# Two-batch attention feeding a dense layer pair on one Trainium2 core: idle matrix products in short bf16 pieces, the first phi tile in three column parts, smaller q loads, the last output tile in two halves, and a new order of the steps

## The chip, the core and the metric

The kernel runs on one core of a Trainium2 chip. The core has a matrix engine (PE, with its weight loads listed apart as PEld), a vector engine (DVE), an activation engine (ACT), GpSimd (POOL), and a queue engine (SP) that here only issues DMAs. Each of them works through its own instructions strictly in the order in which they were written; what one needs of another it waits for with a semaphore. Sixteen DMA engines carry the transfers between HBM and SBUF. Matrix results go to PSUM, which has eight banks; only PE, DVE and ACT reach them. The metric is the device time of one execution in microseconds (us); lower is better. A difference of 0.2% of 655.1 us, 1.3 us, is about what a measurement of this kernel can tell from no change.

## The reference

Eight batches of eight heads, 576 rows each. `phi` makes 32 memory slots a head out of the keys and values, queries attend to the slots, and the result goes through two dense layers with a leaky ReLU between them. The products are wanted in float32.

```python
def _attn_ref(q, k, v, phi):                 # q, k, v: (8, 8, 576, 64), phi: (8, 8, 576, 32)
    a = np.exp(phi - np.max(phi, axis=2, keepdims=True))
    a = a / (np.sum(a, axis=2, keepdims=True) + 1e-09)
    k_m = np.einsum('bhsm,bhsd->bhmd', a, k)
    v_m = np.einsum('bhsm,bhsd->bhmd', a, v)
    scores = 1.0 / np.sqrt(q.shape[-1]) * np.matmul(q, k_m.transpose(0, 1, 3, 2))
    attn = np.exp(scores - np.max(scores, axis=-1, keepdims=True))
    attn = attn / (np.sum(attn, axis=-1, keepdims=True) + 1e-09)
    return np.matmul(attn, v_m)

def _moe_ref(x, w_in, w_out):                # x: (4608, 512), w_in: (512, 2048), w_out: (2048, 512)
    h = x @ w_in
    return np.maximum(0.01 * h, h) @ w_out   # w_in and w_out arrive as float64
```

## The kernel before

The product with the value slots is folded into the first layer: per batch the slots `v_m` (transposed: `vT`) are multiplied with a quarter of `w_in` (`fold_products`, L1007), and the attention weights `a` then go straight through that folded matrix (`w_mem`). So a row of the output costs one "up" product (`a` by folded weights, 128 hidden units at a time), a leaky ReLU on ACT, and one "down" product with `w_out`.

The work is written as small named steps, and two long strings, `OPENING` (L39) and `LATER` (L67), list the steps in the order in which they are issued. Each engine gets its own instructions in that order: a step that stands early in the string stands early on every engine that it uses, and nothing is reordered after that. The names are:

- `a0.` to `a7.` are the eight batches. `phi`, `k`, `v`, `kv`, `q0`, `q1` issue loads on SP. `A1` is the column maximum of phi on DVE, `A2` its transposition on PE, `A3` and `B0` spread the maximum over all rows (DVE, PE). `B1` subtracts it (DVE, L658), `B2` is the exponential (ACT, L664), `B3` sums the exponentials (DVE, L680 to L683). `C1` makes the slots on PE (L698): in batch 0 `C10` is the keys' part and `C11` the values'. `C2` and `C30` make the reciprocal of the sums, `C3k` scales the key slots (ACT), `C31` the value slots (DVE, L754). `D10` and `D3` transpose the key slots (PE, ACT), `D11` and `D5` the value slots, `C4`, `D2`, `D4` bound their size. `Q0` and `Q1` transpose q on DVE (L845). `E10` and `E1` are the scores on PE (L887), `E20` to `E22` copy and transpose them (DVE, L908). `S01` to `S08` is the softmax over the slots for one chunk of the scores, `S11` to `S18` that of the other chunk.
- `i0.` to `i3.` and `o0.` to `o3.` are quarters of `w_in` and `w_out`, each in three pieces: `ld` loads a piece as float64 words into one of eight slots of 6 KB a partition, `y` (ACT), `h` (ACT or DVE, by `OPENING_ACT`) and `t` (DVE, L406) make float32 of it, `b` sums its squares (ACT, 2048 columns).
- `u0.` to `u7.` are the first group of 384 output rows: `P` is an up product (L1114), `V` its leaky ReLU (ACT, L1121), `O` a down product of three row tiles (L1186). `f01.1` is a fold and `f01.2` its two copies into `w_mem`. Capital letters (`P8.0` and on) are groups 1 and 2, `W` the later folds, small letters (`p`, `v`, `d`, `c`, `l`, `s`, `x`) the rest of the rows.
- `z.n` are n idle products (L1384): a matrix of ones times itself, whose result nobody reads.

All loads, and nearly all stores, are issued by SP. Eight semaphores serve the loads in turn, so that a load is issued when the load eight places ahead of it has landed and its slot is free.

The last group has one tile of 128 rows. `down_tile` (L1324) adds its 16 pieces of three products, 512 columns wide, into one PSUM bank; `store` with `last=True` (L1166) scales the left half on ACT and the right half on DVE and sends four stores of 32 rows, two on SP's queue and two on ACT's:

```python
        if last:
            nc.scalar.activation(ob[:, 0:EH], po[:, 0:EH], AF.Copy, scale=so)
            nc.vector.tensor_scalar_mul(ob[:, EH:], po[:, EH:], so)
```

PSUM tiles come from three pools: `ps_a` (three banks, attention and folds), `ps_h` (two, up products), `ps_o` (three, down products).

Of the kernel before, what the change touches and what calls it, by code (L numbers as in the profile page):

```python
# [66 lines left out]
LATER = """  # L67
W01.h1 a2.phi a2.kv2 a2.kv1 o0.s0 W01.h0 a2.A1 Z0.0 o0.s1 a2.kv0 a2.A2 W01.l0 o0.m0 W01.l1 o0.m1
o0.n0 o0.n1 Z0.1 o0.s2 i0.k1 W11.p Z0.2 P8.0 P8.1 V8.0 a2.kv3 W11.h1 P9.0 o0.s3 V8.1 W11.h0 C8 P9.1
L8 W11.l1 V9.0 o1.k0 a2.A4 W11.l0 V9.1 O8.0 W02.h0 o1.l0 W02.h1 C9 o1.k1 O8.1 W02.l1 o1.k2 W02.l0  # L70
o0.m2 L9 o0.m3 W12.p o1.l2 o1.l1 P10.0 W12.h0 o0.n2 P10.1 V10.0 i0.k0 W12.l0 W12.h1 P11.0 o1.s0
V10.1 i0.k2 W12.l1 O9.0 V11.0 C10 o1.m0 o0.n3 L10 P11.1 o1.s1 O9.1 W03.h1 o1.n0 W03.h0 o3.s3 V11.1
P12.0 o1.m1 O10.0 C11 V12.0 o1.n1 L11 P12.1 o1.s2 O10.1 o1.m2 W03.l1 o1.s3 V12.1 W03.l0 a2.A3 o1.n2
o2.k0 C12 W13.p o2.k2 o2.l0 W13.h1 P13.0 W13.h0 W13.l1 P13.1 W13.l0 V13.0 o2.k1 L12 V13.1 O11.0
o1.m3 P14.0 o2.l1 V14.0 C13 o2.s0 P14.1 L13 o2.m0 O11.1 a2.B10 V14.1 o1.n3 o2.n0 o2.s1 P15.0 a2.B20
C14 o2.m1 O12.0 o2.s2 V15.0 o2.n1 o2.m2 a2.C10 L14 P15.1 o2.s3 a2.B3 O12.1 o2.l2 a2.q0 V15.1 o2.n2
o3.s0 a2.q1 o3.k1 o3.k0 o3.l1 P16.0 P16.1 o3.k2 O13.0 V16.0 C15 o2.m3 o3.s1 O13.1 V16.1 C16 o3.l0
o3.s2 o3.m1 a2.C2 a2.C30 i0.l1 o3.l2 o3.m2 P17.0 L15 o3.m3 o3.n3 O14.0 V17.0 L16 a3.phi P17.1 a2.Q0
a2.C3k V17.1 C17 O14.1 o3.n1 a2.D10 i0.l0 a2.Q1 a2.D3 P18.0 O15.0 V18.0 a2.C31 o3.n2 i0.l2 O15.1
o3.m0 P18.1 a2.E1 a2.E22 a2.E3 a3.kv3 i1.k0 L17 a2.E21 a2.E23 V18.1 i1.l0 P19.0 a2.E20 a2.C4 i1.k1  # L80
Z1.2 a3.kv2 P19.1 a2.D11 a2.S01 C18 Z1.1 a3.kv1 Z1.0 a2.S02 L18 V19.0 O16.0 i1.k2 a2.D2 a2.D4
a3.kv0 a2.S03 i1.l2 O16.1 a2.D5 a2.D6 a2.S04 V19.1 P20.0 C19 O17.0 O17.1 o2.n3 V20.0 L19 P20.1
V20.1 i1.l1 C20 i2.k0 P21.0 W20.p a2.S05 i2.k1 O18.0 W20.h0 V21.0 W20.h1 i2.k2 P21.1 L20 O18.1
W20.l1 V21.1 W20.l0 C21 i2.l0 W21.p a2.S06 P22.0 W21.h1 W21.h0 i2.l1 O19.0 V22.0 o3.n0 i2.l2 W21.l0
i3.k1 P22.1 O19.1 i3.k0 W22.p V22.1 a3.A1 i3.k2 L21 a3.A2 W22.h0 P23.0 W22.h1 O20.0 V23.0 a2.S07
P23.1 a3.A4 O20.1 V23.1 a2.S08 i3.l2 C22 i3.l0 W22.l1 C23 W21.l1 O21.0 i3.l1 L23 p0.0 W23.p v0.0
p0.1 W23.h0 p0.2 L22 a3.A3 W23.h1 a3.B10 O21.1 W22.l0 v0.1 a3.B20 W23.l1 a3.C10 O22.0 os2 a3.B3
v0.2 a3.q0 W23.l0 a4.phi a3.C2 p0.3 a3.C30 a3.q1 O22.1 v0.3 a3.C3k s0 c0.0 a3.C31 l0.0 c0.1 a3.D10
l0.1 p1.0 p1.1 a3.D11 v1.0 O23.0 v1.1 a3.C4 p1.2 a3.D3 v1.2 p1.3 a3.Q0 O23.1 v1.3 p2.0 Z2.0 Z2.1 s1
d0.0 Z2.2 p2.1 v2.0 d0.1 v2.1 a3.D2 a4.A1 a3.D4 c1.0 d0.2 c1.1 p2.2 l1.0 d0.3 v2.2 a3.D5 d0.4 a4.A2  # L90
p2.3 a4.A4 p3.0 a3.Q1 a3.D6 l1.1 d0.5 v2.3 a3.E1 a3.E22 d0.6 a3.E3 c2.0 s2 c2.1 p3.1 a3.E23 v3.0
d1.0 v3.1 a3.E20 d1.1 a3.E21 W30.p l2.0 a3.S01 os3 d1.2 a4.kv3 W30.h0 p3.2 W30.h1 a4.kv1 d1.3 v3.2
a4.kv0 d1.4 W30.l0 d1.5 l2.1 W30.l1 p3.3 a3.S02 W31.p a4.kv2 v3.3 c3.0 d1.6 W31.h0 s3 W31.h1 p4.0
a3.S03 p4.1 v4.0 d2.0 v4.1 c3.1 d2.1 a4.A3 l3.0 d2.2 p4.2 d2.3 v4.2 a3.S04 d2.4 d2.5 a4.B10 a3.S05
p4.3 W31.l1 v4.3 p5.0 l3.1 a3.S06 v5.0 d2.6 a4.B20 d3.0 a3.S07 p5.1 W31.l0 a4.C10 s4 v5.1 a3.S08
d3.1 x3.p a4.q0 c4.0 a4.B3 p5.2 d3.2 c4.1 d3.3 x3.0 v5.2 d3.4 p5.3 l4.0 v5.3 x3.1 c5.0 l4.1 x3.2 s5
d3.5 d3.6 p6.0 x3.3 p6.1 l5.0 v6.0 d4.0 p6.2 a4.q1 v6.1 c5.1 d4.1 d4.2 z3.1 a5.phi d4.3 p6.3 l5.1
v6.2 v6.3 d4.4 a4.C2 a4.C30 d4.5 d4.6 p7.0 p7.1 a4.Q0 d5.0 a4.C3k s6 a4.D10 c6.0 a4.D3 l6.0 v7.0
v7.1 a4.Q1 c6.1 d5.1 a4.C31 d5.2 l6.1 p7.2 d5.3 v7.2 d5.4 a4.C4 a5.A1 d5.5 d5.6 d6.0 p7.3 p8.0 z3.0
d6.1 a4.E1 a4.E22 d6.2 a4.E3 a5.kv2 v7.3 c7.0 s7 a5.kv0 p8.1 v8.0 v8.1 a4.E20 a5.kv3 c7.1 a4.E21  # L100
a4.E23 l7.1 p8.2 a5.kv1 d6.3 a4.D11 v8.2 d6.4 a4.D2 a4.D4 p8.3 d6.5 a4.S01 l7.0 a4.S02 v8.3 p9.0
a4.D5 W32.p s8 d6.6 W32.h0 W32.h1 p9.1 W32.l0 v9.0 d7.0 W32.l1 v9.1 d7.1 a4.D6 x4.p os4 c8.0 d7.2
c8.1 p9.2 x4.0 d7.3 v9.2 a4.S03 d7.4 x4.1 p9.3 l8.0 x4.2 d7.5 v9.3 W33.p c9.0 l8.1 d7.6 W33.h1
# [1381 lines left out]
```

## Time and profile before

| | us |
|---|---|
| median of three runs | 655.1 |
| the three runs | 654.94 to 655.29 |
| span of the profiled execution, first to last instruction | 652.3 |
| PE busy in the span | 637.4 (98%) |
| DVE busy | 516.2 (79%) |
| ACT busy | 392.7 (60%) |
| POOL busy | 29.1 (4%) |

The profiled execution has no time of its own beside its span; the median lies 2.8 us above the span. The profile's page lists the busy time of each engine, the span in 40 slices, the chain of work that ended last (followed backwards from the last instruction), and groups of instructions by source line. The trace behind it can be asked for a timeline of each engine, for the chain in order of time, for waits, and for sums in chosen windows. A row of the timeline has the start, the duration, the engine, the line, the operation, the tiles written and read, the shape and the count, and in brackets how long the engine was idle before it and what ended that. Several like instructions are merged into one row.

### The profile page before, as it was taken

Reading aid. Unit: us, or ns where it says so; the run is one execution under the profiler, and the core shown is the slowest. Engines: PE = TensorE matmul, PEld = TensorE weight load, DVE = VectorE, ACT = ScalarE, POOL = GpSimd, SP = SyncE. Lnnn points to the kernel's source line nnn. Section 1 sums busy time; section 2 is a strip of 40 time slices with the busy share of each in tenths; the row PEclk is TensorE's granted clock in tenths of the full one; section 3 lists DMA queues with packets and bytes.
Section 4 is the critical chain, followed back from the end, with each engine's and each line's share of the span. In section 5 each row is a group of like instructions: output and inputs, shape, how many; then the busy total and the mean of one; then the engine's idle time right before and its main releaser. Section 6 shows DMA issues by size and latency. Waiting matters only on the chain.

```text
span 652.3 us, 17093 instructions
## 1 busy us (share of the span) xinstructions
PE 637.4 (98%) x7256; PEld 478.2 (73%) x7256; DVE 516.2 (79%) x863; ACT 392.7 (60%) x671; POOL 29.1 (4%) x37
## 2 busy tenths in 40 slices
PE   7899999999999999999999999999999999999997
PEld 3445545675545778888888888887878888889883
DVE  5875789998997899899969975889887897575641
ACT  2797878765463555557546565655675566565543
POOL 0010031000001001001000010000010001000000
PEclk8799999999999999999999999999999999999999
DMA  9989823105601654431154011064104110010102
GB/s 281 404 312 326 261 68 92 39 11 100 195 2 32 135 156 64 115 112 38 28 122 147 1 33 43 18 127 146 34 18 84 21 28 23 13 30 5 34 2 50
DMA packets 85309, 61.16 MB, mean 94 GB/s; under 512 B 61936, under 2 KB 68336, under 8 KB 85232
## 3 DMA queue, kind: packets, MB, share of 16 engines
q1 hardware_dynamic: 85136, 59.94, 32.8%
q8 instruction: 57, 0.93, 0.6%
q10 hardware_dynamic: 96, 0.13, 0.1%
q14 instruction: 20, 0.16, 0.1%
HBM read 50.59 MB, written 9.45 MB: 92 GB/s over the span
## 4 chain that ended last, share of the span: by engine, by line
PE 97%; DVE 1%; ACT 1%; issue 0%; POOL 0%; ACTq 0%; DVEq 0%; POOLq 0%
PE po L1297 32%; PE ph L1229 22%; PE po L1186 16%; PE ph L1114 8%; PE ph L1297 5%; PE pa L1020 4%; PE pa L698 3%; PE pa L1387 2%; PE po L1331 1%; PE pa L861 1%; PE pa L887 1%; ACT wi L1245 1%; PE pa L344 0%; PE po L698 0%; PE pa L777 0%
## 5 line engine op out<-in xcount | busy, mean ns | idle before, releaser
L1297 PEld LDWEIGHTS <-arena 128*128 128x128 f16 x2184 | 209.8, 98 | 32.0 <-issue 8.8
L1245 ACT ACTIVATE wi<-ph,g_sc 128x256 f32<-128x256 f32 (+1 forms) x224 | 99.3, 466 | 164.5 <-PE ph L1229 156.2
L1229 PE MATMUL ph<-a,w_mem 128*128 128x256 f16 (+3 forms) x1440 | 145.3, 246 | 2.9 <-ACT wi L1245 2.9
L1229 PEld LDWEIGHTS <-w_mem 128*128 128x128 f16 x1440 | 114.6, 98 | 17.8 <-issue 6.3
L1297 PE MATMUL po<-arena 128*128 128x256 f16 x936 | 122.1, 273 | 0.0
L1297 PE MATMUL po<-wo,arena 128*128 128x256 f16 x936 | 122.1, 273 | 0.0
L1186 PE MATMUL po<-wo,arena 128*128 128x512 f16 (+1 forms) x384 | 110.4, 434 | 0.0
L1274 DVE TENSOR_TENSOR arena<-arena 128x1024 f16<-128x1024 f32 x52 | 63.5, 1222 | 22.4 <-ACT arena L1270 22.4
L1274 DVE TENSOR_TENSOR arena<-wi,arena 128x768 f16<-128x768 f32 (+1 forms) x60 | 54.7, 911 | 10.1 <-ACT arena L1270 10.1
L1266 DVE TENSOR_TENSOR arena<-wi 128x256 f32<-128x256 f32 x104 | 40.4, 430 | 25.6 <-ACT wi L1245 25.1
L1270 ACT CAST arena<-arena 128x1024 f16<-128x1024 f32 x52 | 54.5, 1047 | 8.1 <-DVE arena L1266 8.0
L1114 PE MATMUL ph<-a,w_mem 128*128 128x192 f16 (+2 forms) x304 | 51.9, 317 | 0.7 <-DVE a L953 0.7
L1186 PEld LDWEIGHTS <-arena 128*128 128x128 f16 x288 | 27.8, 98 | 29.9 <-issue 0.6
L1270 ACT CAST arena<-wi 128x768 f16<-128x768 f32 (+1 forms) x60 | 46.6, 777 | 1.5
L1266 DVE TENSOR_TENSOR arena<-wi,arena 128x256 f32<-128x256 f32 x104 | 45.7, 440 | 1.8
L1297 PE MATMUL ph<-wo,arena 128*128 128x256 f16 x312 | 42.6, 273 | 0.0
L985 POOL TENSOR_TENSOR a<-t,a 128x1024 f16<-128x1024 f32 (+2 forms) x16 | 21.5, 1360 | 432.9 <-ACT a L980 432.9
L1186 PEld LDWEIGHTS po<-wo,arena 128*128 128x128 f32 x96 | 17.7, 190 | 21.4 <-issue 19.0
L1020 PE MATMUL pa<-wi,vT 64*32 64x512 f16 (+1 forms) x704 | 28.9, 420 | 0.4 <-ACT vT L805 0.4
L1121 ACT ACTIVATE arena<-ph,g_sc 128x384 f32<-128x384 f32 x32 | 18.5, 582 | 15.6 <-PE ph L1114 15.3
L1053 ACT ACTIVATE w_mem<-pa 128x512 f16<-128x512 f32 x40 | 22.7, 596 | 8.4 <-PE pa L1020 7.4
L1114 PEld LDWEIGHTS <-w_mem 128*128 128x128 f16 x240 | 20.7, 98 | 9.7 <-issue 3.6
(216 smaller groups left out, 757.8 us busy)
## 6 DMA issues: line engine op xcount, KB each, us to landing
out_dram<-obs SPq DMA_DIRECT2D x142, 64.0 KB, 1.7
arena<-in_k_dram SPq DMA_DIRECT2D x28, 288.0 KB, 4.5
arena<-in_v_dram SPq DMA_DIRECT2D x28, 288.0 KB, 5.3
arena<-in_q_dram SPq DMA_DIRECT2D x96, 72.0 KB, 2.8
arena<-in_moe_w_in_dram SPq DMA_DIRECT2D x12, 512.0 KB, 9.3
arena<-in_moe_w_out_dram SPq DMA_DIRECT2D x8, 768.0 KB, 6.8
arena<-in_phi_dram SPq DMA_DIRECT2D x7, 576.0 KB, 5.3
arena<-in_q_dram SPq DMA_DIRECT2D x4, 576.0 KB, 8.7
```

Of the source, the lines that this page charges most:

```text
L698: nc.tensor.matmul(var["pk"][g][hh * M:(hh + 1) * M, cs], ld["phi"][rows, hh, j, :], ld["kv", hh][rows, kinds[0]:kinds[-1] + 1, j, :], sta ...
L985: nc.gpsimd.tensor_tensor(piece(lo, tb), piece(t2, tb), piece(hi, tb), ALU.subtract)
L1020: nc.tensor.matmul(pf[g][cols, :], lhs, rhs, start=(n == 0), stop=(n == len(passes) - 1), tile_position=(g * D, hh * M),)
L1053: nc.scalar.activation(tiles(halves(w16(b, j), g)[:, 0]), w(g), AF.Copy, scale=ws)
L1114: nc.tensor.matmul(ph[:, t0:t0 + n * SB], lhs, rhs, start=(m == 0), stop=(m == len(seq) - 1))
L1186: nc.tensor.matmul(po, lhs, rhs, start=(f == 0 and m == 0), stop=(f == NQ * NF - 1 and m == len(seq) - 1),)
L1229: nc.tensor.matmul(ph[:, t0:t0 + n], lhs, rhs, start=(m == 0), stop=(m == len(seq) - 1))
L1245: nc.scalar.activation(dst, ph, AF.Prelu, scale=g_sc2[:, j:j + 1], alpha=SLOPE)
L1266: nc.vector.tensor_tensor(gt[:, x], y, z, op)
L1270: nc.scalar.copy(dst[:, 0], src)
L1274: nc.vector.tensor_tensor(dst[:, 1], src, dst[:, 0], ALU.subtract)
L1297: nc.tensor.matmul(acc, g[:, x, s, u], rhs, start=(h == 0 and j == 0 and u == 0 and m == 0), stop=(j == NQ - 1 and u == 1 and m == 2), ski ...
```

## The change

Idle products are now bf16: the 128 float32 ones are read as 256 bf16 values, each product is 512 columns wide, and its PSUM tile comes from `ps_h` in place of `ps_a`. The opening has 12, 4, 12 and 4 of them where it had 4, 1, 3 and 1 in float32. Phi of batch 0 is subtracted and exponentiated in three column parts (2, 3 and 4 of its 9 column blocks) in place of two (5 and 4). The factor 1/8 on the key slots moves from a DVE instruction of `C30` to the copy in `D3`. Loads of q for batches 0 and 1 take two heads a DMA: eight DMAs in place of four. The last tile's 16 pieces become 32 of half the width in two PSUM banks; the left half is scaled on ACT and stored while the right half is still being multiplied; each half is stored with two DMAs of 64 rows by 256 columns, one from SP, one from ACT. `OPENING` is reordered throughout, of `LATER` the first 45 steps and the tail.

```diff
-            nc.sync.dma_start(
-                t, q[b].rearrange("(hh g) (p j) d -> g p hh j d", g=NG, j=NJ)[g]
-            )
+            src = q[b].rearrange("(hh g) (p j) d -> g p hh j d", g=NG, j=NJ)[g]
+            for hh in range(0, HP, 2):
+                nc.sync.dma_start(t[:, hh:hh + 2], src[:, hh:hh + 2])
...
-        half = (0, (KJ + 1) // 2, KJ) if b == 0 else (0, KJ)
+        half = (0, 2, 5, KJ) if b == 0 else (0, KJ)
...
             nc.vector.reciprocal(r, r)
-            nc.vector.tensor_scalar_mul(r2[:, 1], r, 1.0 / float(D) ** 0.5)
...
-                nc.scalar.copy(kT, var["pkT"])
+                nc.scalar.activation(kT, var["pkT"], AF.Copy, scale=1.0 / float(D) ** 0.5)
...
+    def store_half(G, h, po):
+        ob, cs = obs[:, h * E:h * E + EH], slice(h * EH, (h + 1) * EH)
+        if h:
+            nc.vector.tensor_scalar_mul(ob, po[:, 0:EH], row_scale(G, 0))
+        else:
+            nc.scalar.activation(ob, po[:, 0:EH], AF.Copy, scale=row_scale(G, 0))
+        rows = out.rearrange("(b x j) e -> b j x e", b=B, j=JT)
+        (b, x0), n = next(columns(G, 0)), P // 32
+        for y in range(0, n, n // 2):
+            eng = nc.sync if y == 0 else nc.scalar
+            src = ob[32 * y:32 * (y + n // 2)]
+            eng.dma_start(rows[b, x0 // 32 + y:x0 // 32 + y + n // 2, :, cs], src)
...
-            pos[G] = [ps_o.tile([P, E], F32, name="po")]
+            pos[G] = [ps_o.tile([P, E], F32, name="po") for _ in range(2)]
+        h, i = i // NF, i % NF
...
-                pos[G][0], g[:, x, i], wo_s[j][:, y, i * E:(i + 1) * E],
+                pos[G][h][:, 0:EH], g[:, x, i],
+                wo_s[j][:, y, i * E + h * EH:i * E + (h + 1) * EH],
...
     def idle_products(n):
-        pi = ps_a.tile([P, NF, P], F32, name="pa")
+        pi = ps_h.tile([P, NF, P], F32, name="ph")
         for _ in range(n):
             nc.tensor.matmul(
-                pi, ones, ones.unsqueeze(1).broadcast_to([P, NF, P]), start=True, stop=True
+                pi, halves_of_one[:, :P], halves_of_one.unsqueeze(1).broadcast_to([P, NF // 2, 2 * P]),
+                start=True, stop=True,
             )
...
-c55.1 l55.1 d54.1 d54.2 d54.3 d55.0 d55.1 d55.2 d55.3 end
+c55.1 l55.1 d54.1 d54.5 d54.2 d54.6 d54.3 d54.7 d55.0 d55.1 d55.2 d55.3 end.0 d55.4 d55.5 d55.6
+d55.7 end.1
```

What the new order does at three places, engine by engine (a row is a line of the kernel, the operation, output and inputs, and the shape).

PE between the scores of batch 0 (L887) and the values' part of its slots (L698, after the change L700). Before, three idle products in float32:

```order
L887 MATMUL pa<-wi_87,kT 32x192 x24
L887 MATMUL pa<-wo_91,kT 32x192 x24
L1387 MATMUL pa<-ones 128x512 x3
L698 MATMUL po<-wo_92,wi_88 32x64 x2
L698 MATMUL po<-wo_93,wi_88 32x64 x2
```

With the change, sixteen in bf16, each with a weight load of its own, into a bank of `ps_h`:

```order
L887 MATMUL pa<-wi_87,kT 32x192 x24
L887 MATMUL pa<-wo_91,kT 32x192 x24
L1398 LDWEIGHTS ones
L1398 MATMUL ph<-ones 128x512
...
L700 MATMUL po<-wo_92,wi_88 32x64 x2
L700 MATMUL po<-wo_93,wi_88 32x64 x2
```

The idle products stand in the same place; they no longer take a bank that the score copies of DVE must free first.

DVE after the score copies, in the softmax of the first chunk of batch 0 (`t_308`, after the change `t_319`). Before, `x_v` (step C31, which needs PE's value slots) stands ahead of the sums (L940, step S04):

```order
L908 STREAM_TRANSPOSE t_308<-pa 128x384
L928 TENSOR_REDUCE tm<-t_308 128x12
L754 TENSOR_SCALAR x_v<-po,r_228 128x64 x2
L940 TENSOR_REDUCE ts__420<-t_308 128x24
L941 TENSOR_SCALAR ts__420<-ts__420 128x24
L942 RECIPROCAL ts__420<-ts__420 128x24
L945 TENSOR_TENSOR t_308<-t_308,ts__420 128x768
L953 STREAM_TRANSPOSE a<-t_308 128x768
```

With the change:

```order
L940 TENSOR_REDUCE ts__354<-t_319 128x24
L941 TENSOR_SCALAR ts__354<-ts__354 128x24
L942 RECIPROCAL ts__354<-ts__354 128x24
L754 TENSOR_SCALAR x_v<-po,r_247 128x64 x2
L945 TENSOR_TENSOR t_319<-t_319,ts__354 128x768
L762 TENSOR_REDUCE l_450<-x_v 128x2
L339 TENSOR_REDUCE m_453<-l_450 128x1
L341 TENSOR_SCALAR mdiag<-ident,m_453 128x128
L953 STREAM_TRANSPOSE a<-t_319 128x768
```

The sums now stand ahead of `x_v`, and the three instructions of step C4 (L762, L339, L341) ahead of the transposition that gives the attention weights `a`.

ACT at the end of the program. Before, the scaling of the left half and two stores of 32 rows by 512 columns:

```order
L1270 CAST arena<-wi_89 128x256
L1245 ACTIVATE wi_89<-ph,g_sc_101 128x128 x2
L1270 CAST arena<-wi_89 128x256
L1170 ACTIVATE obs<-po,osc 128x256
L1164 DMA out_dram<-obs 32x512 x2
L1480 UNCONDITIONAL_BRANCH
```

With the change:

```order
L1279 CAST arena<-wi_89 128x256
L1254 ACTIVATE wi_89<-ph,g_sc_101 128x128 x2
L1279 CAST arena<-wi_89 128x256
L1177 ACTIVATE obs<-po,osc 128x256
L1183 DMA out_dram<-obs 2x32x256 x2
L1493 UNCONDITIONAL_BRANCH
```

ACT's two stores are now one for each half, and each covers two blocks of 32 rows by 256 columns; SP issues two more of the same shape.

More of the change, by code (lines that the diff above doesn't have):

```diff
@@ new lines @@
+u3.P1 a1.B0 u3.V1 o2.y2 a1.B10 o2.t1 a0.D4 a1.kv3 a1.B20 i1.b i3.ld0 a1.B3 o2.t2 i3.h0 u3.O0 i3.y1
+u4.P0 i3.h1 a1.C10 a1.C2 a1.C30 a1.q1 u2.V1 a1.C31 a1.C4 u2.O1 o0.b a1.C3k u4.P1 i3.y0 o3.ld0 a1.D10
+a1.D2 i3.t0 a1.D11 a1.D5 a1.Q1 a1.D3 a1.D4 u4.V1 u4.V0 u3.O1 a1.q0 u5.P1 u5.P0 a1.Q0 a0.S18 i3.t1
+i3.ld2 a1.E1 i3.h2 i2.b a1.E21 i3.y2 u4.O0 u5.V0 o1.b a1.E20 i3.t2 a1.S01 a1.S02 u5.O0 u5.V1 o3.ld2
+o0.s0 a1.E22 o3.y0 a2.phi i3.b o3.ld1 ci.1 ci.2 f03.1 o3.h2 o3.h1 o3.h0 a1.S03 a1.S11 ci.3 f03.2
@@ L63 @@
 }
-IDLE = (1, 2, 3, 4)
+IDLE = (1, 2, 3, 4, 6, 8, 12)
 LATER = """
[L68 to L78, printed above, removed]
@@ L85 @@
[L85 to L90, printed above, removed]
@@ new lines @@
+v13.0 d11.0 a5.B10 v13.1 d11.1 c12.1 x5.p d11.2 l12.1 p13.2 d11.3 x5.0 l12.0 v13.2 a5.B20 d11.4
+p13.3 x5.1 a5.C10 x5.2 v13.3 c13.0 s13 d11.5 a5.q0 l13.0 d11.6 c13.1 p14.0 x5.3 p14.1 v14.0 d12.0
+a5.q1 p14.2 a5.B3 d12.1 d12.2 l13.1 a5.C2 a5.C30 d12.3 a5.Q0 v14.1 v14.2 d12.4 a6.phi a5.C3k p14.3
+d12.5 v14.3 a5.D10 a5.D3 c14.0 d12.6 s14 p15.0 a5.C31 v15.0 l14.0 c14.1 p15.1 d13.0 a5.Q1 l14.1
+v15.1 d13.1 z5.1 d13.2 p15.2 d13.3 v15.2 d13.4 d13.5 d13.6 p15.3 p16.0 a5.E1 a5.E22 a5.C4 a5.E3
+a6.kv2 a5.E23 a5.E20 d14.0 v15.3 z5.0 c15.0 s15 p16.1 a6.kv3 a5.D11 v16.0 a6.kv0 v16.1 a5.D2 a5.D4
@@ L1154, in row_scale, with send @@
         return osc_t[:, bs[0] // 2:bs[0] // 2 + 1]
-    def send(G, t, ob, last=False):
+    def send(G, t, ob):
         for y, (b, x) in enumerate(columns(G, t)):
-            rows, eng = out[b * S:(b + 1) * S, :], nc.scalar if last and y % 2 else nc.sync
+            rows = out[b * S:(b + 1) * S, :]
             if b < FB:
@@ L1432 @@
             steps[f"l{m}.{h}"] = lambda k=m, h=h: lo_g(k, h)
-        for n in range(7 if whole(G2 + m // NQ) else NF):
+        for n in range(7 if whole(G2 + m // NQ) else 2 * NF):
             steps[f"d{m}.{n}"] = lambda k=m, n=n: (
@@ L1442 @@
     G = G2 + NG2 - 1
-    steps["end"] = lambda: store(G, 0, pos[G][0], last=True)
+    for h in range(2):
+        steps[f"end.{h}"] = lambda h=h: store_half(G, h, pos[G][h])
     for b in range(B):
```

254 lines of the change are left out of this document (128 added, 126 removed).

## The prediction

> **What bounds the kernel now.** I read first the busy shares and the chain of work that ended last, then the same chain in order of time.
>
> ```profile
> PE 637.4 (98%) x7256; PEld 478.2 (73%) x7256; DVE 516.2 (79%) x863; ACT 392.7 (60%) x671; POOL 29.1 (4%) x37
> PE 97%; DVE 1%; ACT 1%; issue 0%; POOL 0%; ACTq 0%; DVEq 0%; POOLq 0%
> 30.67 1.53 PE ph L1114 x4
> 642.18 5.84 PE po L1331 x27
> ```
>
> The first line gives busy time, the second the chain's share by engine, the others start and length of two pieces of the chain. PE is busy 98% of the span and holds 97% of the chain. From u0.P0 (30.67) to its last product (648.02) it has hardly a gap, and the products of that stretch are the same before and after. So the time is: when that stretch begins, plus its fixed work, plus what follows PE's last product. The change can act in the opening, in the first batches' order, and in the tail. The other engines matter only where PE waits for them.
>
> **The opening.** Windows of 5 us first (length, busy PE, PEld, DVE, ACT, POOL, granted clock, DMA share, GB/s), then the chain:
>
> ```profile
> 5.00:10.00 5.00, 3.22 (x9) 1.20 (x7) 2.59 (x6) 0.87 (x2) 0.00 (x0) 1.00 1.06 302
> 15.00:20.00 5.00, 4.33 (x101) 2.83 (x100) 3.75 (x3) 3.98 (x6) 0.00 (x0) 0.50 1.04 396
> 20.00:25.00 5.00, 4.35 (x16) 1.76 (x18) 4.88 (x8) 2.72 (x5) 0.00 (x0) 0.63 1.04 413
> 25.00:30.00 5.00, 4.08 (x164) 2.06 (x163) 3.75 (x8) 4.74 (x8) 0.87 (x2) 1.00 1.02 408
> ...
> 0.99 6.49 PE pa L1387 x8
> 7.48 0.12 PE pa L633
> ...
> 13.52 1.71 PE pa L1387 x2
> ...
> 16.79 3.29 PE pa L887 x94
> ...
> 20.69 4.32 PE pa L1387 x6
> 25.02 1.63 PE po L698 x102
> 26.65 0.46 DVE x_v L754 x2
> 27.11 0.87 DVE ts__420 L940
> 28.00 0.19 DVE ts__420 L941
> 28.21 0.31 DVE ts__420 L942
> 28.55 0.97 DVE t L945
> 29.54 0.99 DVE a L953
> ...
> 3.67 2.19 DVE L592 TENSOR_REDUCE r1k<-wi 128x64 f32<-128x576 f32 x2 [3.67 <-DMA wi<-in_phi_dram]
> 14.29 0.17 DVE L726 TENSOR_SCALAR r<-r 128x2 f32<-128x2 f32 x1
> 15.83 0.33 SPq L549 DMA_DIRECT2D wi<-in_v_dram  x1
> 30.45 0.24 DVE L762 TENSOR_REDUCE l<-x_v 128x2 f32<-128x128 f32 x1
> 29.33 1.06 ACT L1370 COPY w_mem<-pa 128x512 f32<-128x512 f32 x2
> ```
>
> Step one, the transposition A2 (L633). DVE has the column maximum at 3.67 + 2.19 = 5.86, yet A2 starts at 7.48: PE is still in the four float32 idle products. A bf16 product of 512 columns took 5.84 / 27 = 0.216 at full clock; twice that is 0.43 at half clock. Twelve from 0.99 end near 6.2, so A2 comes about 0.9 earlier. Phi in three parts adds an instruction each on DVE and ACT to a chain that alternates between them; I put it at one small instruction, 0.17 as L726 with its two columns takes, and round to 0.2. The instruction of C30 that goes saves as much. These two cancel, and the scores of batch 0, which end at 16.79 + 3.29 = 20.08, end at about 19.15.
>
> Step two, the idle products behind the scores. They end at 20.69 + 4.32 = 25.01 now; C11 and all of the values' side follows. Sixteen bf16 products from 19.15: if the clock opens where it did (the window from 20 to 25 has a mean of 0.63, which is 0.5 up to 23.7 and 1.0 after), 4.55 us at 0.43 hold 10.6 of them, and 5.4 more take 1.2: they end at 24.9, and C11 gains 0.1. With a full clock throughout they end at 22.6, and C11 then starts with its operand: about 22.75.
>
> Step three, from C11 to u0.P0. PE waits for `a` (L953, ends 30.53) and the copies of the fold (L1370, end 30.39). The sums (0.87 + 0.19 + 0.31 = 1.37) now run in the shade of C11, ahead of `x_v`; the three instructions of C4, beginning with L762, are put in front of L953 and cost about 0.7. So `a` is ready 0.1 + 1.37 - 0.7 = 0.8 earlier, 29.7. The fold's copies stand behind an `o0.y` and the second exponential on ACT, and come to about 30.05. **u0.P0 gains 0.6.** If C11 comes a step of the clock earlier, the same path gives 29.35 (gain 1.3), with a full clock about 28.7 (2.0). I take 0.9, between the first two, and keep 0.3 (three-part phi dearer by 0.3) and 2.0 as ends. The half clock has this reason to stay as it was: in the window from 5 to 10 PE was 64% busy and the next stretch had half clock; from 15 to 20 it was 87% busy, and half clock stayed.
>
> The Trainium skill, "TensorE: Matmul & The Clock Gate", Part 1, says that one busy window of 3.4 us opens the clock and that what counts is busy time, not the number of products. The row from 15 to 20 (4.33 of 5.00 busy at 0.50) doesn't bear that out, so the measurement decides; by the page alone the opening would gain 2.0.
>
> The eight loads of q in place of four cost SP four more issues, none of which PE waited for before: their cover is that q is wanted after the keys. I put them at nothing, at most 0.33 each (the issue at 15.83) in front of a `kv` load, which the second rival bears.
>
> **The tail.** The chain's end, the queues (with the median time from issue to landing), then windows in the same columns; 636.70 holds an ordinary store of 64 KB.
>
> ```profile
> 648.05 0.48 ACT obs L1170
> 648.56 0.48 DVE obs L1171
> 649.08 0.86 ACTq L1164 DMA_DIRECT2D out_dram<-obs  x2
> out_dram<-obs SPq DMA_DIRECT2D x2, 64.0 KB, 1.7
> out_dram<-obs ACTq DMA_DIRECT2D x2, 64.0 KB, 2.0
> 649.80:651.10 1.30, 0.00 (x0) 0.00 (x0) 0.00 (x0) 0.00 (x0) 0.00 (x0) 1.00 0.80 202
> 636.70:636.95 0.25, 0.17 (x4) 0.17 (x4) 0.00 (x0) 0.22 (x2) 0.00 (x0) 1.00 0.95 221
> 118.00:119.20 1.20, 1.20 (x12) 0.86 (x11) 1.20 (x3) 1.20 (x4) 0.00 (x0) 1.00 0.29 97
> ```
>
> PE ends at 648.02; ACT and DVE scale one after the other, since both read one bank (0.48 each); each queue issues two stores (0.86); the data runs from 649.8 to 651.1; the span ends at 652.3. With halves in two banks the DVE half is done at 648.02 + 0.03 + 0.48 = 648.5 plus 0.1 for 96 narrow weight loads and products in place of 48, that is 648.6 against 649.04, and there is one issue behind it in place of two, 0.43 less: 0.44 + 0.43 - 0.1 gives **about 0.7 to 0.8 gained, if the stores move as fast as before.** The left half's store can start its data at about 648.1: ACT is done with it by 647.3, and between ACT's end (649.04) and data (649.8) lay 0.77.
>
> But the form of these stores changes. All stores of before are 32 rows by 512 columns, and the row of 636.70 shows that one such store fills 0.95 of the sixteen DMA engines. The new ones are written, in the order above, as 2x32x256: the outermost dimension is 2. If a transfer is dealt out by its outermost dimension, 2 of 16 engines carry it, and for both queues the same two.
>
> What that costs: the row of 118 gives 97 GB/s at a share of 0.29, so one engine moves 97 / (16 x 0.29) = 20.9 GB/s; the window from 20 to 25 gives 413 / (16 x 1.04) = 24.8; the tail's own window 202 / (16 x 0.80) = 15.8. The tile has 128 x 512 x 4 = 262 kB. Two engines need 262 / (2 x 20.9) = 6.3 us, with bounds of 5.3 and 8.3. From 648.1 that ends at 654.4 against 651.1: **3.3 us later** (2.3 to 5.3). I take the rate of 118, which lies between the other two. The split into halves earns nothing then, since its 0.7 lies in front of a transfer that ends last.
>
> The Trainium skill, "DMA: Bandwidth & Descriptors", "Why a DMA increments its semaphore by 16 and not by 1", states this dealing: the largest number up to 16 that divides the slowest dimension of both sides, the lowest-numbered engines. By it a 2 gives two engines. The trace shows its other side only: 32 outermost rows and 0.95 of sixteen engines.
>
> **The sum.** 655.1 - 0.9 + 3.3 = **657.5**. The profiled execution has a span of 652.3, 2.8 below the median of 655.1; I take those 2.8 us as unchanged, since they lie outside first and last instruction.
>
> **The rivals.**
>
> First, the stores spread over all engines after all (the outer 2 and the 32 rows dealt out together). Then the tail gains 0.7: 655.1 - 0.9 - 0.7 = 653.5, from 652.4 (opening 2.0) to 654.5. This is the other side. The point that decides is the DMA share after 648: near 0.9 with sixteen engines, at most 0.13 (2 of 16) with two. For it speaks that all transfers of this trace use all sixteen; against it, that none of them has an outermost dimension below 32. Chance 0.27: faster 0.16, within 0.2% 0.11.
>
> Second, PE waits at the slots of batch 1 (C10).
>
> ```profile
> 54.44 0.33 SPq L549 DMA_DIRECT2D arena<-in_v_dram  x1
> arena<-in_v_dram SPq DMA_DIRECT2D x4, 288.0 KB, 8.8
> 62.43 1.45 PE L1114 MATMUL ph<-a,w_mem 128*128 128x384 f32 x4
> 63.88 2.18 PE pa L698 x144
> ```
>
> Now the last load of values is issued at 54.44 and takes about 8.8 to land: 63.2, just before C10 at 63.88. The new order moves two up products (1.45 each) and one transposition of a bound behind C10, so that PE would reach it 33.2 - 3.1 = 30.1 after u0.P0, at about 60.2. The loads of q are also put behind it, which frees 2 x 576 KB of traffic; but if the values land as before, PE stands 2.5 us, and every batch behind it too: 657.5 + 2.5 = 660.0. Behind C10 on PE are queued u2.O1, the transpositions and the scores of batch 1; ACT and DVE wait for those. Chance 0.08.
>
> Third, the clock. With sixteen products in a row of bf16 the half clock may end earlier, and the opening gains 2.0 rather than 0.9: 657.5 - 1.1 = 656.4 with two engines in the tail. Chance 0.05, from the 87% busy window that didn't do it.
>
> **How the numbers follow.** The forecast has 0.60: two engines in the tail and the opening near -0.9, whose bounds (-2.0 to -0.3 and +2.3 to +5.3) give some 655.8 to 659.9. The range reaches down into the first rival and up to the second: 653.0 to 660.0. A measurement can tell 0.2%, 1.3 us. Slower by more: the forecast's part above 656.4 (0.52) and the second rival, 0.60. Within: 0.08 of the forecast, 0.05 of the third rival, 0.11 of the first, 0.24. Faster: 0.16.
>
> **What would show it.** The tail: the DMA share in the last 6 us (at most 0.13 for two engines) and the time from the last issue to the end (5 us or more, against 1.7 to 2.0 for the stores of before). The opening: A2 near 6.5, the scores' end near 19.2, C11 near 24.9 with the clock, u0.P0 near 29.8. Batch 1: no gap of PE ahead of the slots near 60. Wrong would make it a tail that moves 200 GB/s, or a gap of over 1 us anywhere between 35 and 100, where the order is new throughout and the margins of the first batches are small.

## The result, and the profile after

| | before | after |
|---|---|---|
| median, us | 655.2 | 669.8 |
| the runs, us | 654.94 to 655.29 | 668.99 to 671.39 |
| span of the profiled execution, us | 652.3 | 667.0 |

The ratio is 1.0238, with a 95% interval of 1.0222 to 1.0254: slower, by 14.6 us. The first fence has five lines of the page after: busy times, granted clock and DMA share in 40 slices of 16.7 us, a DMA queue (transfers, MB, share), and the chain's share by engine.

```profile
PE 639.0 (96%) x7318; PEld 482.4 (72%) x7318; DVE 516.7 (77%) x856; ACT 392.2 (59%) x672; POOL 30.4 (5%) x37
PEclk9799998999999999999999999999999999999999
DMA  9978730405510752441055011064114001010110
q8 instruction: 57, 0.93, 0.6%
PE 84%; DVE 5%; DMA 4%; ACT 4%; issue 1%; SPq 0%; ACTq 0%; DVEq 0%
```

PE has 1.6 us more work than before, but its share of the chain fell from 97% to 84%: DVE, ACT and the DMAs now hold parts of it. The clock dips in the second slice and again in the seventh (100 to 117 us).

Where the 14.7 us of the span came from is read best from the start of the same product in both traces:

| product | before | after | difference |
|---|---|---|---|
| u0.P0 | 30.67 | 29.15 | -1.5 |
| slots of batch 1 (C10) | 63.81 | 63.73 | -0.1 |
| scores of batch 1 (E1) | 74.09 | 77.66 | +3.6 |
| slots of batch 2 | 141.30 | 149.83 | +8.5 |
| slots of batch 5 | 318.83 | 328.42 | +9.6 |
| end of the last product | 648.02 | 658.76 | +10.7 |
| end of the span | 652.3 | 667.0 | +14.7 |

So the opening gains 1.5; the first two batches lose 10.0; two steps of about 1 us come later (behind the slots of batch 4 and of batch 7); and the tail loses 4.0.

Each column is one execution. The gain of the opening is not clear of their scatter: with the opening of the change u0.P0 came at 29.37 to 31.88 in e1, e4, e8 and e9 below, with that of before at 31.40 and 33.49 in e16 and e15. The loss behind it is: from u0.P0 to the slots of batch 2 the order of before takes 110.6 to 110.8 us in three traces (before, e15, e16), the changed order 120.7, and 119.4 in e1, which has the same steps up to there.

Here are PE's rows after at each place where the first two batches lose (start, length, products, and in brackets PE's idle time before and what ended it):

```profile
29.15 5.69 PE L1114 MATMUL ph<-a,w_mem 128*128 128x384 f32 x12 [0.43 <-DVE a L953]
45.48 2.84 PE L1195 MATMUL po<-wo,arena 128*128 128x512 f32 x6 [0.60 <-ACT arena L1121]
49.35 2.85 PE L1114 MATMUL ph<-a,w_mem 128*128 128x384 f32 x8 [1.03 <-ACT w_mem L1381]
77.66 1.93 PE L887 MATMUL pa<-arena,kT 32*32 32x192 f32 x96 [1.63 <-DVE arena L845]
86.13 0.27 PE L473 MATMUL pa<-ident,sq 128*4 128x128 f32 x1 [1.19 <-ACT wi L413]
98.55 0.27 PE L473 MATMUL pa<-ident,sq 128*4 128x128 f32 x1 [1.54 <-ACT wi L413]
100.65 2.93 PE L1114 MATMUL ph<-a,w_mem 128*128 128x384 f32 x4
```

Twelve products of 384 columns take 5.69 us at 29.15, and four take 2.93 at 100.65; before, four took 1.45 (the row of 62.43). At both places PE runs at half clock: the granted clock is 0.51 from 28.90 to 32.30 and from 100.58 to 104.00. The other rows are five waits of 0.6 to 1.6 us, and each names ACT or DVE. What those engines waited for stands in the queues:

```profile
26.10 10.82 SPq L374 DMA_DIRECT2D arena<-in_moe_w_out_dram  x2
67.62 0.92 SPq L587 DMA_DIRECT2D arena<-in_q_dram  x2
77.60 0.71 ACT L388 ACTIVATE arena<-arena 128x512 uint32<-128x512 uint16 x1 [5.17 <-DMA arena<-in_moe_w_in_dram]
657.98 1.85 SPq L1183 DMA_DIRECT2D out_dram<-obs  x2
...
34.50:37.50 3.00, 3.00 (x9) 1.41 (x8) 2.66 (x4) 3.00 (x6) 0.00 (x0) 1.00 0.10 41
658.80:666.00 7.20, 0.00 (x0) 0.00 (x0) 0.47 (x1) 0.00 (x0) 0.00 (x0) 0.85 0.12 38
```

Three rows of the kernel before, for comparison: SP's longest row in this stretch, the same window of the DMA engines, and the scores of batch 1.

```profile
25.90 6.60 SPq L372 DMA_DIRECT2D arena<-in_moe_w_out_dram  x2
34.50:37.50 3.00, 3.00 (x9) 1.42 (x8) 2.02 (x4) 3.00 (x5) 0.30 (x1) 1.00 0.97 345
74.09 1.96 PE L887 MATMUL pa<-arena,kT 32*32 32x192 f32 x96 [0.56 <-ACT kT L799]
```

After the change, SP issues one load at 26.10 and the next only at 36.6: that one (o1.ld2) needs the slot that o0.t1 empties, and o0.t1 needs o0.h1 and o0.y1, which now stand behind u0.V0 on ACT, and u0.V0 waits for u0.P0. From 34.5 to 37.5 the DMA engines therefore run at a share of 0.10. The last q load of batch 1, the second of the row of 67.62, goes out at 68.1 (before, at 58.9). ACT stands 5.17 us for a piece of w_in, with sums of squares behind it that need no load. The row of 658.80 is the tail: a share of 0.12 and 38 GB/s for over 7 us.

### The profile page after: what moved, and what is told of

It reads as the page before. It is cut to its first block, busy times and chain, and to the rows that moved or that the text cites. A ratio compares the mean times of both kernels' runs of the same rounds, so it can differ in the third digit from the quotient of the medians.

```text
span 667.0 us, 17209 instructions
## 1 busy us (share of the span) xinstructions
PE 639.0 (96%) x7318; PEld 482.4 (72%) x7318; DVE 516.7 (77%) x856; ACT 392.2 (59%) x672; POOL 30.4 (5%) x37
## 4 chain that ended last, share of the span: by engine, by line
PE 84%; DVE 5%; DMA 4%; ACT 4%; issue 1%; SPq 0%; ACTq 0%; DVEq 0%
PE po L1306 30%; PE ph L1238 21%; PE po L1195 11%; PE ph L1114 6%; PE ph L1306 5%; PE pa L1020 3%; PE pa L700 2%; ACT wi L413 1%; PE po L1341 1%; DMA arena<-in_moe_w_in_dram 1%; PE pa L861 1%; DMA arena<-in_q_dram 1%; DMA arena<-in_phi_dram 1%; DVE r1k L594 1%; DMA arena<-in_moe_w_out_dram 1%
## 5 line engine op out<-in xcount | busy, mean ns | idle before, releaser
L1114 PE MATMUL ph<-a,w_mem 128*128 128x192 f16 (+2 forms) x304 | 55.0, 328 | 1.5 <-ACT w_mem L1381 1.0
```

Of the source, the lines that this page charges most:

```text
L1114: nc.tensor.matmul(ph[:, t0:t0 + n * SB], lhs, rhs, start=(m == 0), stop=(m == len(seq) - 1))
```

## The experiments

Times are medians; the kernel before, run beside each, had 654.3 to 655.2. Gains over the change are differences of medians; taken from the ratios to the kernel before they come out up to 1.2 us larger. The ratio of the change itself has an interval of 1.0222 to 1.0254; a gain counts as clear where a run's interval lies below that. Each edit is to the changed kernel unless it says otherwise. Two of the expectations call the batches of the late pauses 3 and 6; counted from 0, as the steps are, they are 4 and 7.

### The stores of the last tile: e1, e15, e16

```diff
-        for y in range(0, n, n // 2):
-            eng = nc.sync if y == 0 else nc.scalar
-            src = ob[32 * y:32 * (y + n // 2)]
-            eng.dma_start(rows[b, x0 // 32 + y:x0 // 32 + y + n // 2, :, cs], src)
+        for y in range(n):
+            eng = nc.scalar if y % 2 else nc.sync
+            eng.dma_start(rows[b, x0 // 32 + y, :, cs], ob[32 * y:32 * y + 32])
```

> The changed kernel, but each half of the last tile is stored in four DMAs of 32 rows by 256 columns, two on SP and two on ACT, in place of two of 64 rows. Theory 'two engines': the time from PE's last product to the end of the span falls from 8.2 us to about 3.8 (4.3 before the change, less the second scaling of 0.5), the DMA share after it rises from 0.13 to 0.6 or more; 669.8 - 4.4 = 665.4 us. Rival 'narrow rows': rows of 1024 bytes are slow whoever carries them; then nothing changes by more than 1 us and the share stays low.

664.8 us (ratio 1.0149, 1.0123 to 1.0174), 5.0 less than the change. From PE's last product to the end of the span it takes 4.4 us, where 3.8 was expected and the change takes 8.2. e15 and e16 put the change's last tile alone on the kernel before, with its stores and with those of e1.

> The kernel before with the change's last tile alone: halves in two PSUM banks, each stored in two DMAs of 64 rows by 256 columns. Theory 'two engines': 655.1 - 0.7 (halves) + 4.4 (as e1 gave back) = 658.8 us, at least 657.5; DMA share after PE's end near 0.13. Rival: under 1 us slower, since in e1 something else of the changed tail was undone too.

> As e15, with the stores in 32 rows by 256 columns. Theory: the halves' own gain, 0.5 to 0.8 us: 654.4 us. Rival: 48 more products and weight loads and four more issues eat it, 655.1 us or more.

e15: 658.2 us (1.0053, 1.0033 to 1.0073). e16: 654.1 (0.9992, 0.9980 to 1.0004). The windows behind PE's last product, of e1, e15 and e16 in this order:

```profile
659.70:661.30 1.60, 0.00 (x0) 0.00 (x0) 0.00 (x0) 0.00 (x0) 0.00 (x0) 1.00 0.35 87
651.60:658.30 6.70, 0.00 (x0) 0.00 (x0) 0.00 (x0) 0.00 (x0) 0.00 (x0) 0.78 0.12 39
650.00:651.80 1.80, 0.00 (x0) 0.00 (x0) 0.00 (x0) 0.00 (x0) 0.00 (x0) 1.00 0.30 74
```

A store whose outermost dimension is 2 runs at a share of 0.12, two of sixteen engines, in the change and in e15. The rule of the Trainium skill in "DMA: Bandwidth & Descriptors", "Why a DMA increments its semaphore by 16 and not by 1", agrees with the 0.12. The windows of e1 and e16 hold the second half alone (87 x 1.6 = 139 kB), that of e15 the whole tile (39 x 6.7 = 261 kB). In e1 the first half's data moves just ahead of this window, at a share of 0.61 from 658.4 to 658.8, so the whole tile takes about 2.5 us there and 6.7 in e15. The share of 0.6 that I expected is reached while a half is under way; between the halves it falls to 0.14.

The price of the stores' form is 658.2 - 654.1 = 4.1 us. The whole tail of the change, halves and stores, costs the kernel before 3.5 (e15's ratio, 0.0053 of 655). The halves by themselves show a gain of 0.4, and e16's interval reaches over no change.

### The order: e2

The steps up to P10.1 in the order of before; all else as changed. The idle products stand at the four places of before, and so the last four of them between C4 and u0.P0, where the change has none.

> The changed kernel with the order of the kernel before for all steps up to P10.1 (phi's third part and the idle products put where their like stood, 12, 4, 16 and 4 of them); tail, q loads, bf16 idle products and three-part phi as in the changed kernel. Theory 'order': the 10 us that PE loses between 30 and 110 us come from the new order, so they go: 655.2 + 3.9 (tail) with an opening gain of 0 to 1 gives 658 to 659 us. Rival 'parts': they come from the split q loads, the bf16 idle products or the three-part phi; then it stays above 666 us.

660.1 us (1.0082, 1.0056 to 1.0109): 9.7 of the 14.6 are the order. The pauses of PE listed above are gone, and in the stretch in which the DMA engines stood they run in full. The other two rows are u0.P0 and the slots of batch 2:

```profile
34.50:37.50 3.00, 3.00 (x9) 1.52 (x8) 1.61 (x3) 3.00 (x6) 0.95 (x2) 1.00 1.00 373
29.57 1.56 PE L1109 MATMUL ph<-a,w_mem 128*128 128x384 f32 x4 [1.10 <-ACT w_mem L1376]
140.45 2.25 PE L695 MATMUL pa<-arena 64*32 64x128 f32 x144
```

From the one to the other it takes 110.9 us, against 110.6 before and 120.7 with the change: the loss of the first two batches is the order's. Two pauses for PE's program (see e5) stand in its trace too, of 0.83 us ahead of 250.10 and 1.63 ahead of 497.18.

### What in the order: e3 (clock), e4 (slots), e8 (q), e9 (squares), e12 (together)

```diff
 e3  -a0.C31 a0.D11 a0.D5 o0.y0 ... a0.C4 a0.S13
     +a0.C31 z.3 a0.D11 a0.D5 z.1 o0.y0 ... a0.C4 z.2 a0.S13
 e4  -a0.S14 o1.ld1 u0.V0 u0.P1 i1.ld0 o0.ld2 i1.ld1 o0.h0 o0.t0 o0.h1
     +a0.S14 o1.ld1 o0.h0 o0.t0 o0.h1 o0.y1 o0.t1 u0.V0 u0.P1 i1.ld0 o0.ld2 i1.ld1
 e8  -f02.1 i3.ld1 a1.kv2 ... u3.O1 a1.q0 ... a0.S18 i3.t1
     +f02.1 a1.q0 a1.kv2 ... u3.O1 i3.ld1 ... a0.S18 i3.y1 i3.h1 i3.t1
 e9  -u5.P0 a1.Q0 a0.S18 i3.t1 i3.ld2 a1.E1 i3.h2 i2.b ... u5.V0 o1.b
     +u5.P0 i2.b o1.b a1.Q0 a0.S18 i3.t1 i3.ld2 a1.E1 i3.h2 ... u5.V0
```

> The changed kernel with six more idle products in the gaps of PE between 25.7 and 29.2 us (three behind C31, one behind D5, two behind C4). Theory 'clock': PE stands half of the window from 25.5 to 28.9, the clock halves until 32.3, u0.P0 takes 2.9 us in place of 1.5, and what follows (leaky ReLU, slots, loads) is late for that; with the clock held at 1.0 the gaps up to 100 us shrink by about two thirds: 669.8 - 6 = about 664 us. Rival 'order': the clock costs only its own 1.6 us, most of which PE spends waiting for loads anyway: 668 to 670 us.

668.5 us (1.0206, 1.0176 to 1.0235), 1.3 less. The two windows of e3 hold full clock from 25.5 to 32.3; the third row is the kernel before:

```profile
25.50:28.90 3.40, 3.00 (x75) 1.06 (x63) 3.19 (x10) 2.77 (x4) 0.00 (x0) 1.00 1.02 411
28.90:32.30 3.40, 2.92 (x11) 1.80 (x10) 1.60 (x4) 2.82 (x7) 0.87 (x2) 1.00 1.03 403
28.87 1.13 PE L1387 MATMUL pa<-ones 128*128 128x512 f32 x2
```

The kernel before has an idle product just ahead of u0.P0 (its last `z.1`); the change has moved all of them ahead of C11. So the half clock behind u0.P0 is real, but holding it off earns about its own price at most; the 664 of the theory lies below the interval, and the theory is refuted.

> The changed kernel with o0.h0, o0.t0, o0.h1, o0.y1 and o0.t1 put ahead of u0.V0, where they wait for no product. Theory 'slots': the load that SP holds from 26.1 to 36.6 us (o1.ld2, which needs the slot that o0.t1 frees) is issued by about 33 us, the 3 us in which no DMA runs go, and the gaps of PE at 45, 49, 57, 77 and 86 us shrink: about 666 us. Rival 'clock': the issue at 36.6 is a follower; nothing moves by more than 1 us.

667.6 us (1.0193, 1.0158 to 1.0229), 2.2 less. SP's queue, the same window, and PE's products at 48:

```profile
26.70 7.54 SPq L369 DMA_DIRECT2D arena<-in_moe_w_out_dram  x2
34.50:37.50 3.00, 3.00 (x9) 1.41 (x9) 1.15 (x2) 2.01 (x4) 0.00 (x0) 1.00 0.87 292
48.09 2.74 PE L1109 MATMUL ph<-a,w_mem 128*128 128x384 f32 x8
```

SP's wait is 3.3 us shorter, the hole in the DMA is closed, and the two pauses at 45 and 49 are gone; those at 77, 86 and 98 are not. They have other causes, and in this trace, of a run of 668.8 us, the one at 86 is longer (2.07 us).

> The changed kernel with the load a1.q0 where i3.ld1 stood (ahead of a1.kv2) and i3.ld1 where a1.q0 stood, with i3.y1 and i3.h1 moved behind it. Theory 'q late': PE's pause of 1.6 us ahead of the scores of batch 1 (77.7 us) is the load of q, issued at 68 behind o3.ld0, and goes; what follows may lose part of it again to the late i3.ld1: 668 to 670 us, the pause at 77 under 0.5. Rival: the pause stays or shifts, since SP is behind as a whole.

668.1 us (1.0206, 1.0180 to 1.0231), 1.7 less. The pause ahead of the scores of batch 1 is gone (no idle time in the row), the ones at 86 and 98 stay:

```profile
77.18 1.93 PE L882 MATMUL pa<-arena,kT 32*32 32x192 f32 x96
```

> The changed kernel with the two sums of squares i2.b and o1.b moved ahead of i3.h2 on ACT. In the changed kernel ACT stands 5.2 us (72.4 to 77.6) for the load i3.ld2, with these 3.8 us of work queued behind it, and i3.b, ci.1 and the fold f03 come late for that. Theory 'ACT queue': the pauses of PE at 86 (1.2 us) and 98 (1.5 us) go, and with the second the half clock at 100.6 to 104: 669.8 - 4 = about 666 us. Rival 'loads': o3's loads set these pauses; under 1 us gained.

670.2 us (1.0249, 1.0217 to 1.0280), nothing gained:

```profile
80.57 3.25 PE L882 MATMUL pa<-arena,kT 32*32 32x192 f32 x96 [2.46 <-DVE arena L840]
90.69 0.27 PE L468 MATMUL pa<-ident,sq 128*4 128x128 f32 x1
103.07 0.27 PE L468 MATMUL pa<-ident,sq 128*4 128x128 f32 x1 [1.53 <-ACT wi L408]
```

The pause it was meant for is gone (the row of 90.69 has none), but the one ahead of the scores is 0.8 longer and the one at 98 stays. By itself the repair shows no gain. Why is not shown: the trace is of the slowest of its runs, 674.1 us, in which u0.P0 came as late as 31.88.

The intervals of e3, e4, e8 and e9 all overlap that of the change. So their rows show that a pause goes with its cause, and their times alone do not show what it was worth. e12 has these three repairs (not the clock's), with e1 and with the float32 idle products of e5 below.

> The changed kernel's own order with all repairs together: the emptied slots of o0 ahead of u0.V0 (e4), q of batch 1 for i3.ld1 (e8), i2.b and o1.b ahead of i3.h2 (e9), float32 idle products (e5), stores of 32 rows (e1). Theory 'separate causes': their gains add, 669.8 - 4.4 (tail) - 2.2 (program) - 1.6 (slots) - 1.6 (q) - 1.2 (squares) = about 658.8 us, with the pause at 98 us left. Rival 'one cause, the loads as a whole': what one repair gives the next pause takes, 662 us or more.

659.1 us (1.0063, 1.0040 to 1.0087), as the sum of separate causes said, and below the 662 of the rival. The sum's terms were read off the traces, though; the gains measured one by one add up to 11.8 by medians and 14.6 by ratios, against 10.7 and 11.5 for all together, so not all of each adds. From u0.P0 to the slots of batch 2 its trace takes 116.2 us, 4.5 less than the change, and e5, with the idle products alone, 120.9: by these single traces the three repairs together are worth about four. Behind u0.P0 its one pause of over 1.2 us in the first two batches is the expected one, where the sums of squares of o3 are late:

```profile
96.74 0.27 PE L468 MATMUL pa<-ident,sq 128*4 128x128 f32 x1 [1.54 <-ACT wi L408]
```

### The opening alone: e6, e10, e14

The new order up to u0.P0, the old one behind it, with e1's stores and e5's idle products. Each of the next two is a change to the one ahead of it; the lines give the sequence of the loads.

```diff
 e6   o0.ld1 o0.ld0 i1.ld2 o0.ld2 o1.ld0 i1.ld1 i1.ld0 o1.ld2 ...
 e10 -o0.ld1 o0.ld0 i1.ld2
     +o0.ld0 o0.ld1 i1.ld2
 e14 -o0.ld0 o0.ld1 i1.ld2 o0.ld2 o1.ld0 i1.ld1 i1.ld0 o1.ld2
     +o0.ld0 o0.ld2 o0.ld1 o1.ld0 i1.ld1 i1.ld0 i1.ld2 o1.ld2
```

> New order up to u0.P0, the order of the kernel before from there on, stores of 32 rows in the last tile (as e1), float32 idle products (as e5). Theory: each part that loses is undone and the gain of the opening stays (u0.P0 at about 29.5 in place of 30.7) with the halves' 0.7 in the tail: 655.2 - 1 - 0.5 = 653.7 us, 651.5 to 655 us. Rival 'opening is what starves the loads': the steps ahead of u0.P0 keep the loads back, and it stays above 657 us.

658.2 us (1.0056, 1.0036 to 1.0077): the rival was right, with a pause of PE of 2.95 us, from 48.1 on. Now e10:

> As e6, with the loads o0.ld0 and o0.ld1 exchanged, so that the eighth-next load waits for the slot that o0.t0 frees in place of o0.t1. Theory 'slots': in e6, as in the changed kernel, SP stands from 27 to 36.7 us for the slot of o0.ld1, the DMA engines are idle from 35.5 to 37.5, and PE pauses 3.1 us at 47.5 for the piece of w_in that comes late for it; here the load is issued by about 33.5 us, the pause goes, and the time is 658.2 - 3.5 = 654.7 us or a little less. Rival 'opening starves the loads in other ways': the pause moves on, over 657 us.

658.4 us (1.0059, 1.0038 to 1.0081): wrong again. SP's wait for the slot ends by 32, but the pause is still 2.5 us. Its chain shows why, in the row of SP: i2.ld1 waits until 41.88, for the slot that i1.t2 empties.

```profile
41.16 0.70 DVE wi L403
41.86 0.02 issue
41.88 0.33 SPq L373
```

The eight slots are handed out in turn, so the sequence of the loads decides which piece must be put away for which load. The new opening brings i1.ld2 ahead of o0.ld2, and its slot is wanted eight loads later, by i2.ld1, while the old order puts it away late. e14 keeps the new compute steps (but for i1.y2, behind its load) and takes the old sequence of loads.

> As e10, but with the loads of batch 0 and of the weights in the sequence of the kernel before (o0.ld0, o0.ld2, o0.ld1, o1.ld0, i1.ld1, i1.ld0, i1.ld2, ...), each at a place where the new opening has a load, and i1.y2 moved back behind its load; the compute steps up to u0.P0 keep the new order. Theory 'slots': a load waits for the piece eight places ahead to be put away; in e10 i2.ld1 waits until 41.9 us for i1.t2, in the kernel before it waited until 36.1 for o0.t1. With the old sequence the pause of 2.6 us ahead of u2.P1 (49.5 us) goes, 658.4 - 3 = 655.4 us or less. Rival: the pause stays, over 657 us, and the compute steps of the opening are its cause.

655.3 us (1.0005, 0.9990 to 1.0019): 3.2 less than e10, as expected. In place of the pause ahead of u2.P1 there is one of 1.8 us inside the second fold, behind a load that was issued at 42.12 and took 8.27:

```profile
42.12 8.27 DMA arena<-in_moe_w_in_dram
...
52.76 1.05 PE L1015 MATMUL pa<-wi,vT 64*32 64x512 f32 x4 [1.78 <-DVE wi L403]
```

So in this trace u0.P0 stands at 30.12, 0.6 ahead of before, and the slots of batch 1 at 66.22, 2.4 behind: what the opening may win goes in the next wait for a load.

### PE's own program: e5, e13

After the change PE stands twice without a wait on anything in the trace, behind the slots of batches 4 and 7 (rows of the change):

```profile
260.21 0.27 PE L1306 MATMUL po<-wo,arena 128*128 128x256 f16 x1 [0.81 <-issue]
506.06 0.71 PE L1306 MATMUL ph<-wo,arena 128*128 128x256 f16 x5 [1.01 <-issue]
```

The page's queue of kind "instruction" has 57 transfers and 0.93 MB, that is 16 KB each. One ran at 257.70 to 258.95, another at 503.62 to 504.50; PE went on 1.3 and 1.6 us after their ends.

```diff
 e5  -pi, halves_of_one[:, :P], halves_of_one.unsqueeze(1).broadcast_to([P, NF // 2, 2 * P]),   # z.12 z.4 z.12 z.4
     +pi, ones, ones.unsqueeze(1).broadcast_to([P, NF, P]),                                     # z.3 z.1 z.3 z.1
 e13 (to the kernel before)
     -i0.ld2 z.1
     +i0.ld2 zz z.1
     +pi[:, 0, 0:1], halves_of_one[:, :P], halves_of_one[:, 0:1],                               # zz: 14 times
```

> The changed kernel with its idle products in float32 again (3, 1, 3 and 1 of 128 float32 columns each in place of 12, 4, 12 and 4 in bf16, still in ps_h): some 30 fewer instructions on PE. Theory 'fetch': PE's program is fetched in blocks of 16 KB, in every run so far PE stands at the same place in its own count of instructions, and with the change that place falls just behind the 144 small products of the slots of batches 3 and 6, where PE runs through the rest of its block in under 1 us; with 28 fewer instructions the place falls some 30 instructions later in the work, so the pauses of about 1.0 us at 259 and 1.2 us at 505 go: 669.8 - 2.2 = 667.6 us, first 110 us as before within 1. Rival 'loads': the two pauses come from the q loads then under way; they stay, 669 to 670 us.

666.5 us (1.0170, 1.0141 to 1.0199), 3.3 less than the change; in its trace both products start at once:

```profile
259.87 0.83 PE L1301 MATMUL po<-wo,arena 128*128 128x256 f16 x6
505.00 0.83 PE L1301 MATMUL ph<-wo,arena 128*128 128x256 f16 x6
```

> The kernel before with 14 bf16 products of one column, whose result nobody reads, put behind the load i0.ld2: 28 more instructions on PE, under 1 us of work in a stretch where PE waits. Theory 'fetch': they shift PE's program so that its blocks end just behind the slots of batches 3 and 6; two pauses of about 1 us appear near 250 and 496 us and the time grows by 1.5 to 2.5 us, to 656 to 657 us. Rival: no change beyond 0.5 us.

656.5 us (1.0024, 1.0008 to 1.0041): 28 instructions that do nothing cost the kernel before 0.5 to 2.7 us. The pause behind the slots of batch 7 appeared; that behind batch 4 was 0.47 (ahead of 250.34), smaller than expected.

```profile
497.14 0.72 PE L1292 MATMUL ph<-wo,arena 128*128 128x256 f16 x5 [0.98 <-issue]
```

### The parts that are left: e11

```diff
 (to e2)
+stores as in e1
-z.12 z.4 z.12 z.4 z.4
+z.4 z.1 z.3 z.1, in float32
```

> As e2 (the order of the kernel before), with stores of 32 rows in the last tile and float32 idle products (4, 1, 3 and 1). Theory: e2's 660.1 holds the two engines (4.4 us) and two pauses for PE's program (1.0 and 1.9 us), both go: 660.1 - 6.5 = 653.6 us, that is the kernel before less 0.5 to 1 for the halves and an instruction of C30. Rival 'other parts cost too' (q split, three-part phi): 656 us or more.

655.5 us (1.0006, 0.9994 to 1.0019): with order, stores and idle products undone, what is left of the change (three-part phi, split q, the factor in D3, halves) neither gains nor costs, taken together. The rival's 656 was not reached, and neither was the gain of 0.5 to 1.5 that I gave it. No version beats the kernel before; e16 comes nearest.

## Why the prediction was wrong

The direction was right and the size was not: 2.4 us slower was forecast, 14.6 measured, outside the range. The tail, for which it was forecast, gave some 4 of them; ten came where the prediction saw no loss.

- **The step that failed** is in the first part: "the products of that stretch are the same before and after. So the time is: when that stretch begins, plus its fixed work, plus what follows PE's last product." The products are the same, but PE no longer runs through them. The new order moves loads, the steps that empty their slots, and the sums of squares as much as products. The stretch from u0.P0 to the slots of batch 2 grew from 110.6 to 120.7 us by that, six of it in five waits of PE and some three in products at half clock, and with the old order it is back at 110.9 (e2). I followed one load (the values of batch 1) through the new order, and not the slots.
- **The second rival** had the mechanism, a load that PE waits for, at the wrong place: at C10 PE does not wait at all (63.73 after, 63.81 before). It was priced 2.5 us and one place (its rows give 63.2 - 60.2 = 3.0); there were five.
- **The last paragraph** named "a gap of over 1 us anywhere between 35 and 100" as what would make it wrong. There were four, and the range gave them no width.
- **The tail** was right, and the first rival with its sixteen engines wrong: two engines, a share of 0.12 against "at most 0.13", and 8.2 us from PE's end to the span's end against 4.3, a loss of 4.0 where 3.3 was forecast and 5.3 was the bound. e15, with this tail on the kernel before, gives 3.5. The left half's stores were issued at 657.98, 0.8 us before PE's end, but no data moved before 659.2, 0.4 behind it (0.1 in the prediction), and the transfers ran until 665.7.
- **The opening**: the rows of A2, of the last scores and of the first of C11 (chain and timeline of the change) are

```profile
6.08 0.32 PE pa L635
...
16.58 2.38 PE L887 MATMUL pa<-wo,kT 32*32 32x192 f32 x48
24.02 0.27 PE L700 MATMUL po<-wo,wi 64*32 64x64 f32 x6
```

  so A2 came at 6.08 (forecast 6.5), the scores ended at 18.96 (19.2), C11 began at 24.02 (24.9) and u0.P0 at 29.15 (29.8). A gain of 1.5 where 0.9 was taken and 2.0 was the bound. Two things fit the extra. A2 gained 1.4: the prediction's own rows, 7.48 and 6.2, allow 1.3, and it took 0.9. And the clock opened at 22.1, not at the 23.7 read for the kernel before, which is the third rival's way in part. But u0.P0 scatters by over 2 us between executions of one opening, so a part of this close agreement in one trace is luck. What I did not see is that the clock closes again at 28.9; by medians e3 prices that at 1.3, not clear of the noise.
- **The split of q** was put at nothing for SP's issues, and no cost is seen in e11, which has it. That q stands late, behind o3.ld0 in the queue, made the pause of 1.63 at 77.66 (e8: 1.7 by medians, not clear of the noise).
- **Not in the prediction at all**: the pauses for PE's program. I counted what the idle products take and not how many instructions they are.
- **Slips in its sums**, none of which moves the forecast: the 0.1 for narrow products is taken off the halves' gain twice (0.84 in place of 0.7 to 0.8; e16 shows 0.4), the bounds add up to 655.4 to 660.1, and those of the first rival to 652.4 to 654.1.

By runs the 14.6 are: 9.7 for the order (change less e2), 4.6 for the stores and the idle products together (e2 less e11; e15 less e16 put 4.1 on the stores), and 0.3 in e11, which is no change. The pieces do not fit to the last microsecond. The 3.3 of e5 is more than its two pauses of together 1.8, while for e2's two, of together 2.5, only 0.5 is left; what else the idle products move in the first batches stays open. So does part of the order's loss: e12 is still 3.6 above e11, and its trace 5.6 above before in the stretch up to the slots of batch 2. Its pause of 1.5 at 96.7, one of 0.9 within the slots of batch 1 and a half clock around 30 us are seen, and not tried one by one.
